# One load queue in the order of use, weights cast on VectorE, and an unrolled head of five units, in an HGRN2 attention followed by an MLP

## The chip, the cores and the metric

The kernel runs on one core of one Trainium2 chip. The metric is the device time of one execution in microseconds, and less is better. The engines are named as the profile names them: PE (TensorE, matmuls), DVE (VectorE), ACT (ScalarE), POOL (GpSimd), SP (SyncE, which issues DMAs here).

## The reference

A gated linear attention over 4 batches, 8 heads, 768 steps and a head size of 48, and then an MLP with a leaky ReLU over its 3072 rows of 384:

```python
# q, k, v, f_logit: (4, 8, 768, 48); w_in: (384, 2048); w_out: (2048, 384); all float32
f = 1.0 / (1.0 + np.exp(-f_logit))
state = np.zeros((B, H, D, D))
for t in range(S):
    state = f[:, :, t, :, None] * state + np.einsum('bhd,bhe->bhde', k[:, :, t], v[:, :, t])
    y[:, :, t] = np.einsum('bhd,bhde->bhe', q[:, :, t], state)
x = y.transpose(0, 2, 1, 3).reshape(B * S, H * D)
h = x @ w_in
out = np.maximum(0.01 * h, h) @ w_out
```

## The kernel before

The work is cut into 24 units, one for each chunk of 128 steps and each batch; the chunk is the outer index, so that units 0 to 3 are the first chunk of the four batches. One unit is 128 rows of the MLP's input. A unit goes through these steps, each a function of its own:

- `load(u)`: four DMAs of 192 KB on SP's queue (f, k, q, v, each 128 x 8 x 48 floats, so runs of 192 bytes).
- `gate_act` (ACT, L109 and L111): the negative logarithm of the gate. `gate_pe` (PE, L117 and L120): its running sum over the chunk in `cs`, by a triangular matrix, and four columns of totals. `decay_act` (ACT, L129 to L133): `em_t` and `a_t`, the exponentials of the sum and of its negative, and `a_end`.
- `scale_pool` (POOL, L139 to L142): `kh` = k times `em_t`, `qh` = q times `a_t`, and v in bf16.
- `turn_pe` and `turn_dve`: eight transposes into `tp`, copied to `kT` and to the block-diagonal `qbd` (DVE, L155 to L158).
- `score_pe` and `mask_dve`: scores in two PSUM tiles `pw`, masked into `wm` (DVE, L175).
- `mix_pe`, `y_act`: the unit's output `py` (L187 from the state, L191 within the chunk), copied to `xn` by ACT (L226). `state_pe`, `state_dve`, `state_pool`: the update of the batch's state (L203, L213 to L222).
- `x_pe`, `x_dve`: three transposes of `xn`, copied to `xT` (L233, L238).
- `up(u, g)`, g from 0 to 3: twelve matmuls with `xT` and a quarter of w_in's columns (L250), then the leaky ReLU on ACT into `gT` (L252).
- `down(u, half)`: eight matmuls with `gT` and w_out each (L259). `put(u)`: the copy to `osb` (DVE, L264) and the store on SP's queue.

The order is written out by hand: within an engine instructions run as the program lists them, and across engines they wait for each other's data and for buffers. PSUM tiles come from pools with few buffers: `sm` (`cs`, `py`, `pt` and `px` by turns) has two, `pw` two, `pm` two, `tp` one and `pm2` one.

Weights are loaded by POOL's queue, which casts float32 to bf16 on the way, in eight DMAs that are issued beside the first loads on SP's queue. Inputs are loaded five units ahead. Before the loop the attention of unit 0 is done; turn i of the loop then does the MLP of unit i with the attention of unit i + 1, the gate of unit i + 2 and the gate's logarithm of unit i + 3 between its pieces.

Of the kernel before, what the change touches and what calls it, by code (L numbers as in the profile page):

```python
# [9 lines left out]
FP32 = mybir.dt.float32  # L10
# [5 lines left out]
def kernel(  # L16
# [24 lines left out]
    const = ctx.enter_context(tc.tile_pool(name="const", bufs=1))  # L41
    inp = ctx.enter_context(tc.tile_pool(name="inp", bufs=6))
    work = ctx.enter_context(tc.tile_pool(name="work", bufs=3))
    gpool = ctx.enter_context(tc.tile_pool(name="gpool", bufs=5))
    opool = ctx.enter_context(tc.tile_pool(name="opool", bufs=4))

    ps_m = ctx.enter_context(tc.tile_pool(name="ps_m", bufs=2, space=bass.MemoryType.PSUM))
    ps_o = ctx.enter_context(tc.tile_pool(name="ps_o", bufs=1, space=bass.MemoryType.PSUM))
    ps_t = ctx.enter_context(tc.tile_pool(name="ps_t", bufs=1, space=bass.MemoryType.PSUM))
    ps_w = ctx.enter_context(tc.tile_pool(name="ps_w", bufs=2, space=bass.MemoryType.PSUM))  # L50
    ps_s = ctx.enter_context(tc.tile_pool(name="ps_s", bufs=2, space=bass.MemoryType.PSUM))

# [18 lines left out]
    qbds = [const.tile([128, P2, 2, 128], BF16, name=f"qbd{i}", tag=f"qbd{i}") for i in range(2)]  # L71
    state_f = [const.tile([128, P2, D], FP32, name=f"sf{b}", tag=f"sf{b}") for b in range(B)]
    state_b = [const.tile([128, P2, D], BF16, name=f"sb{b}", tag=f"sb{b}") for b in range(B)]
    for t in lfs + qhs + khs + qbds:
        nc.vector.memset(t, 0.0)
    for t in state_f:
        nc.vector.memset(t, 0.0)


    raw = {}  # L80
# [1 line left out]
    def load(u):  # L82
        c, b = units[u]
        r = {}
        for name, src in (("f", f_logit), ("k", k), ("q", q), ("v", v)):
            t = inp.tile([128, H, D], FP32, name=f"{name}_raw", tag=f"{name}_raw")
            nc.sync.dma_start(out=t, in_=src[b, :, c * C:(c + 1) * C, :].rearrange("h t d -> t h d"))
            r[name] = t
        raw[u] = r

    def load_w_in(part, parts):
        w = FF // parts
        for kk in range(NK):
            nc.gpsimd.dma_start(out=w_in_b[:, kk, part * w:(part + 1) * w],  # L94
                                in_=moe_w_in[kk * 128:(kk + 1) * 128, part * w:(part + 1) * w])

    def load_w_out(part, parts):
        n = NF // parts
        nc.gpsimd.dma_start(  # L99
            out=w_out_b[:, part * n:(part + 1) * n, :],  # L100
            in_=moe_w_out[part * n * 128:(part + 1) * n * 128, :].rearrange("(a p) n -> p a n", p=128))

    st = {}

# [1 line left out]
    def gate_act(u):  # L106
        f = raw[u]["f"]
        e = work.tile([128, H, D], FP32, name="e_t", tag="e_t")
        nc.scalar.activation(e, f, AF.Exp, scale=-1.0)  # L109
        lf = lfs[u % 3]  # L110
        nc.scalar.activation(lf[:, :, 0:D], e, AF.Ln, bias=1.0)  # L111

    def gate_pe(u):
        c, b = units[u]
        lf = lfs[u % 3]
        cs = ps_s.tile([128, 512], FP32, name="cs", tag="sm")
        nc.tensor.matmul(cs[:, 0:H * D], ut, lf[:, :, 0:D], start=True, stop=True)  # L117
        if c < NCH - 1:
            for p in range(P2):
                nc.tensor.matmul(cs[:, H * D + p:H * D + p + 1], lf[:, 2 * p:2 * p + 2, :], ones_col,  # L120
                                 start=True, stop=True)
        st[u] = {"cs": cs}

    def decay_act(u):
        c, b = units[u]
        cs = st[u]["cs"]
        a_t = work.tile([128, H, D], BF16, name="a_t", tag="a_t")
        em_t = work.tile([128, H, D], BF16, name="em_t", tag="em_t")
        nc.scalar.activation(em_t, cs[:, 0:H * D], AF.Exp, scale=1.0)  # L129
        nc.scalar.activation(a_t, cs[:, 0:H * D], AF.Exp, scale=-1.0)  # L130
        if c < NCH - 1:
            a_end = work.tile([128, P2], FP32, name="a_end", tag="a_end")
            nc.scalar.activation(a_end, cs[:, H * D:H * D + P2], AF.Exp, scale=-1.0)  # L133
            st[u]["a_end"] = a_end
        st[u]["a"], st[u]["em"] = a_t, em_t

    def scale_pool(u):
        r = raw.pop(u)
        nc.gpsimd.tensor_mul(khs[u % 3][:, :, 0:D], r["k"], st[u]["em"])  # L139
        nc.gpsimd.tensor_mul(qhs[u % 3][:, :, 0:D], r["q"], st[u]["a"])  # L140
        v_b = work.tile([128, H, D], BF16, name="v_b", tag="v_b")
        nc.gpsimd.tensor_copy(out=v_b, in_=r["v"])  # L142
        st[u]["v"] = v_b

    def turn_pe(u):
        tp = ps_t.tile([128, 2, P2, 128], BF16, name="tp", tag="tp")
        for i, src in enumerate((khs[u % 3], qhs[u % 3])):
            for p in range(P2):
                nc.tensor.transpose(tp[:, i, p, :], src[:, 2 * p:2 * p + 2, :], ident)  # L149
        st[u]["tp"] = tp  # L150

    def turn_dve(u):
        tp = st[u].pop("tp")
        kT = work.tile([128, P2, 128], BF16, name="kT", tag="kT")
        nc.vector.tensor_copy(out=kT, in_=tp[:, 0])  # L155
        qbd = qbds[u % 2]
        nc.vector.tensor_copy(out=qbd[0:64, :, 0, :], in_=tp[0:64, 1])
        nc.vector.tensor_copy(out=qbd[64:128, :, 1, :], in_=tp[64:128, 1])  # L158
        st[u]["kT"] = kT
# [91 lines left out]
                                 start=(kk == 0), stop=(kk == NK - 1))  # L251
        nc.scalar.activation(s["g"][:, 4 * g:4 * g + 4, :], pm, AF.Prelu, alpha=0.01)  # L252

    def down(u, half):
        s = st[u]
        if half == 0:
            s["pm2"] = ps_o.tile([128, KD], FP32, name="pm2", tag="pm2")
        for ff in range(8 * half, 8 * half + 8):
            nc.tensor.matmul(s["pm2"], s["g"][:, ff, :], w_out_b[:, ff, :], start=(ff == 0), stop=(ff == NF - 1))  # L259

    def put(u):
# [3 lines left out]
        nc.sync.dma_start(out=out[b * S + c * C:b * S + (c + 1) * C, :], in_=osb)  # L265
        st.pop(u)


    LA = 5
    load(0)  # L270
    load_w_in(0, 2)
    load(1)
    load_w_in(1, 2)
    load_w_out(0, 2)
    load_w_out(1, 2)
    for u in range(2, LA):
        load(u)

    gate_act(0)
    gate_act(1)  # L280
    gate_pe(0)
    decay_act(0)
    scale_pool(0)
    gate_pe(1)
    decay_act(1)
    scale_pool(1)
    gate_act(2)
    turn_pe(0)
    turn_dve(0)
    score_pe(0)  # L290
    mask_dve(0)
    mix_pe(0)
    state_pe(0)
    y_act(0)
    state_dve(0)
    state_pool(0)
    x_pe(0)
    x_dve(0)

    for i in range(NU):  # L300
        n1, n2, n3 = i + 1, i + 2, i + 3
        if i + LA < NU:
            load(i + LA)
        if n1 < NU:
            turn_pe(n1)
            turn_dve(n1)
        up(i, 0)
        up(i, 1)
        if n1 < NU:
            score_pe(n1)  # L310
            mask_dve(n1)
        if n2 < NU:
            gate_pe(n2)
            decay_act(n2)
            scale_pool(n2)
        up(i, 2)
        up(i, 3)
        if n1 < NU:
            mix_pe(n1)
            y_act(n1)  # L320
            state_pe(n1)
            state_dve(n1)
            state_pool(n1)
        if n3 < NU:
            gate_act(n3)
        down(i, 0)
        if n1 < NU:
            x_pe(n1)
            x_dve(n1)
        down(i, 1)  # L330
        put(i)

# [29 lines left out]
```

## Time and profile before

| | |
|---|---|
| median of 3 runs | 213.21 us (212.39 to 214.24) |
| the profiled execution | 211.29 us, its span 209.4 us |
| PE busy | 177.8 us, 85% of the span |
| DVE, ACT, POOL busy | 97.4, 108.7, 76.8 us |
| SP's queue (inputs, outputs) | 23.60 MB, 59.5% of 16 engines' span |
| POOL's queue (weights; bytes as written) | 3.15 MB, 9.0% |
| granted TensorE clock | 1.00 |

A line of the timeline has the start in us, the duration in us, the engine, the line of the kernel, the operation, the tile written and the tiles read, shapes, and the number of instructions merged in it; in brackets stands how long the engine had been idle and what ended that. A line of the chain of waits has start, duration, engine, tile and line. "x24" are 24 instructions. The page's rows of digits are the busy share of 40 equal slices, in tenths.

### The profile page before, as it was taken

What the parts mean: (1) busy time and instruction counts of PE and PEld (TensorE: products, weight loads), DVE (VectorE), ACT (ScalarE), POOL (GpSimd) and SP (SyncE); (2) the same over time, 40 slices, a digit from 0 to 9 for tenths busy, and PEclk for the clock granted to TensorE, in tenths of its full rate; (3) what the DMA queues carried; (4) which work ended last, traced back from release to release, by engine and by line L of the source; (5) the groups of instructions that cost most, each with busy time, mean ns of one, the idle gap of its engine ahead of it and who ended that gap; (6) DMA issues with size and microseconds to landing.
All of it is one profiled execution on the core that took longest, in us unless ns stands there. A gap on an engine that the chain in (4) does not pass through costs nothing.

```text
span 209.4 us, 5831 instructions
## 1 busy us (share of the span) xinstructions
PE 177.8 (85%) x2432; PEld 146.1 (70%) x2432; DVE 97.4 (46%) x223; ACT 108.7 (52%) x237; POOL 76.8 (37%) x129
## 2 busy tenths in 40 slices
PE   0000149999999999999999999999999999999993
PEld 0000028788779788877988887798888778877881
DVE  8000044466546545654654565465455545633511
ACT  4000332775576458447645845774585567555540
POOL 8300071542553255145325524532552454034000
PEclk9999999999999999999999999999999999999999
DMA  6999999998796479568647846956695681100111
GB/s 114 171 195 184 199 191 189 156 219 163 121 176 143 105 136 177 114 118 163 147 102 133 186 111 116 157 116 141 128 187 113 119 153 41 38 28 18 38 41 38
DMA packets 106267, 27.12 MB, mean 130 GB/s; under 512 B 100352, under 2 KB 105472, under 8 KB 106240
## 3 DMA queue, kind: packets, MB, share of 16 engines
q1 hardware_dynamic: 103296, 23.60, 59.5%
q0 software_dynamic: 2944, 3.15, 9.0%
q8 instruction: 19, 0.31, 0.6%
q14 instruction: 8, 0.07, 0.1%
HBM read 25.17 MB, written 4.72 MB: 143 GB/s over the span
## 4 chain that ended last, share of the span: by engine, by line
PE 83%; issue 10%; POOL 4%; DVE 1%; ACT 0%; POOLq 0%
PE pm L250 32%; PE pm L259 30%; PE pw L168 6%; PE tp L149 5%; PE py L191 2%; PE px L233 2%; PE py L187 2%; PE cs L117 2%; PE pt L203 2%; POOL w_in_b L94 2%; POOL w_out_b L99 1%; POOL kh L139 1%; PE cs L120 1%; DVE wm L175 1%; POOL qh L140 1%
## 5 line engine op out<-in xcount | busy, mean ns | idle before, releaser
L252 ACT ACTIVATE gT<-pm 128x512 bf16<-128x512 f32 x96 | 56.2, 601 | 64.1 <-PE pm L250 62.3
L250 PE MATMUL pm<-xT,w_in_b 128*128 128x128 bf16 x1152 | 73.4, 221 | 0.0
L259 PE MATMUL pm<-w_out_b,gT 128*128 128x384 bf16 x384 | 70.1, 326 | 0.0
L250 PEld LDWEIGHTS <-w_in_b 128*128 128x128 bf16 x1152 | 67.2, 99 | 0.6
L139 POOL TENSOR_TENSOR kh<-k_raw,em_t 128x384 bf16<-128x384 f32 x24 | 22.0, 916 | 110.5 <-ACT em_t L129 105.7
L259 PEld LDWEIGHTS <-gT 128*128 128x128 bf16 x384 | 35.2, 98 | 18.8
L175 DVE TENSOR_TENSOR wm<-pw,ut 128x512 bf16<-128x512 f32 x48 | 30.9, 686 | 12.7 <-PE pw L168 11.9
L117 PE MATMUL cs<-lf,ut 128*128 128x384 bf16 x24 | 8.1, 339 | 24.9 <-ACT lf L111 24.9
L264 DVE COPY osb<-pm 128x384 f32<-128x384 f32 x24 | 13.4, 558 | 26.6 <-PE pm L259 26.6
L109 ACT ACTIVATE e_t<-f_raw 128x384 f32<-128x384 f32 x24 | 12.9, 536 | 23.7 <-DMA f_raw<-in_f_logit_dram 23.7
L120 PEld LDWEIGHTS <-lf 128*128 128x128 bf16 x80 | 5.0, 99 | 25.2 <-issue 23.8
L140 POOL TENSOR_TENSOR qh<-q_raw,a_t 128x384 bf16<-128x384 f32 x24 | 21.9, 914 | 0.0
L155 DVE COPY kT<-tp 128x512 bf16<-128x512 bf16 x24 | 10.0, 415 | 23.6 <-PE tp L149 23.6
L238 DVE COPY xT<-px 128x384 bf16<-128x384 bf16 x24 | 8.6, 358 | 22.2 <-PE px L233 22.2
L213 DVE TENSOR_TENSOR sf<-sf,pt 64x192 f32<-64x192 f32 x20 | 6.9, 346 | 22.2 <-PE pt L203 22.2
L168 PE MATMUL pw<-qbd,kT 128*128 128x256 bf16 x96 | 14.8, 277 | 1.3 <-DVE qbd L158 1.3
L129 ACT ACTIVATE em_t<-cs 128x384 bf16<-128x384 f32 x24 | 11.8, 491 | 4.5 <-PE cs L120 3.7
L111 ACT ACTIVATE lf<-e_t 128x384 bf16<-128x384 f32 x24 | 12.5, 523 | 0.8
L168 PEld LDWEIGHTS <-kT 128*128 128x128 bf16 x96 | 9.4, 99 | 4.3 <-DVE kT L155 0.8
L226 ACT CAST xn<-py 128x384 bf16<-128x384 f32 x24 | 11.4, 474 | 1.5 <-PE py L191 1.5
L142 POOL CAST v_b<-v_raw 128x384 bf16<-128x384 f32 x24 | 12.1, 505 | 0.0
L130 ACT ACTIVATE a_t<-cs 128x384 bf16<-128x384 f32 x24 | 11.6, 485 | 0.0
(37 smaller groups left out, 155.3 us busy)
## 6 DMA issues: line engine op xcount, KB each, us to landing
f_raw<-in_f_logit_dram SPq DMA_DIRECT2D x24, 192.0 KB, 3.2
k_raw<-in_k_dram SPq DMA_DIRECT2D x24, 192.0 KB, 3.8
q_raw<-in_q_dram SPq DMA_DIRECT2D x24, 192.0 KB, 4.0
v_raw<-in_v_dram SPq DMA_DIRECT2D x24, 192.0 KB, 4.3
out_dram<-osb SPq DMA_DIRECT2D x24, 192.0 KB, 2.0
w_in_b<-in_moe_w_in_dram POOLq DMA_DIRECT2D x6, 256.0 KB, 8.8
w_out_b<-in_moe_w_out_dram POOLq DMA_DIRECT2D x2, 768.0 KB, 18.2
```

The lines of the kernel that those rows point to most:

```text
L109: nc.scalar.activation(e, f, AF.Exp, scale=-1.0)
L111: nc.scalar.activation(lf[:, :, 0:D], e, AF.Ln, bias=1.0)
L117: nc.tensor.matmul(cs[:, 0:H * D], ut, lf[:, :, 0:D], start=True, stop=True)
L139: nc.gpsimd.tensor_mul(khs[u % 3][:, :, 0:D], r["k"], st[u]["em"])
L140: nc.gpsimd.tensor_mul(qhs[u % 3][:, :, 0:D], r["q"], st[u]["a"])
L142: nc.gpsimd.tensor_copy(out=v_b, in_=r["v"])
L168: nc.tensor.matmul(pw[:, 2 * i:2 * i + 2, :], kT[:, p, :], qbd[:, p, :, :], start=True, stop=True)
L175: nc.vector.tensor_mul(wm, pw, ut[:, None, :].to_broadcast([128, 4, 128]))
L250: nc.tensor.matmul(pm[:, i, :], w_in_b[:, kk, ff * 128:(ff + 1) * 128], s["xT"][:, kk, :], start=(kk == 0), stop=(kk == NK - 1))
L252: nc.scalar.activation(s["g"][:, 4 * g:4 * g + 4, :], pm, AF.Prelu, alpha=0.01)
L259: nc.tensor.matmul(s["pm2"], s["g"][:, ff, :], w_out_b[:, ff, :], start=(ff == 0), stop=(ff == NF - 1))
L264: nc.vector.tensor_copy(out=osb, in_=st[u]["pm2"])
```

## The change

All loads are issued by SP, in one list. The weights come as float32 into staging tiles, w_in in four quarters of its columns and w_out in two halves of its columns, and DVE casts them into the bf16 tiles. The zeroing of the tiles is shared by DVE and POOL. For the first five units `kh` is made on DVE. `tp` takes its buffers from the pool of `pw`, and `pm2` has two banks. In place of the short prologue there is a head in which five units go through all their steps in an order written out by hand, with the down projection by halves of the output's columns (`down_cols`); the loop then begins at unit 5, whose first turn has an order of its own. Inputs are loaded four units ahead in the loop.

```diff
--- before.py
+++ after.py
@@ -41,12 +41,12 @@
     const = ctx.enter_context(tc.tile_pool(name="const", bufs=1))
     inp = ctx.enter_context(tc.tile_pool(name="inp", bufs=6))
     work = ctx.enter_context(tc.tile_pool(name="work", bufs=3))
-    gpool = ctx.enter_context(tc.tile_pool(name="gpool", bufs=5))
-    opool = ctx.enter_context(tc.tile_pool(name="opool", bufs=4))
+    gpool = ctx.enter_context(tc.tile_pool(name="gpool", bufs=6))
+    opool = ctx.enter_context(tc.tile_pool(name="opool", bufs=6))
+    stage = ctx.enter_context(tc.tile_pool(name="stage", bufs=1))
 
     ps_m = ctx.enter_context(tc.tile_pool(name="ps_m", bufs=2, space=bass.MemoryType.PSUM))
-    ps_o = ctx.enter_context(tc.tile_pool(name="ps_o", bufs=1, space=bass.MemoryType.PSUM))
-    ps_t = ctx.enter_context(tc.tile_pool(name="ps_t", bufs=1, space=bass.MemoryType.PSUM))
+    ps_o = ctx.enter_context(tc.tile_pool(name="ps_o", bufs=2, space=bass.MemoryType.PSUM))
     ps_w = ctx.enter_context(tc.tile_pool(name="ps_w", bufs=2, space=bass.MemoryType.PSUM))
     ps_s = ctx.enter_context(tc.tile_pool(name="ps_s", bufs=2, space=bass.MemoryType.PSUM))
 
@@ -71,10 +71,10 @@
     qbds = [const.tile([128, P2, 2, 128], BF16, name=f"qbd{i}", tag=f"qbd{i}") for i in range(2)]
     state_f = [const.tile([128, P2, D], FP32, name=f"sf{b}", tag=f"sf{b}") for b in range(B)]
     state_b = [const.tile([128, P2, D], BF16, name=f"sb{b}", tag=f"sb{b}") for b in range(B)]
-    for t in lfs + qhs + khs + qbds:
-        nc.vector.memset(t, 0.0)
+    for n, t in enumerate(lfs + khs + qhs + qbds):
+        (nc.vector if n % 2 == 0 else nc.gpsimd).memset(t, 0.0)
     for t in state_f:
-        nc.vector.memset(t, 0.0)
+        nc.gpsimd.memset(t, 0.0)
 
 
     raw = {}
@@ -88,17 +88,26 @@
             r[name] = t
         raw[u] = r
 
-    def load_w_in(part, parts):
-        w = FF // parts
-        for kk in range(NK):
-            nc.gpsimd.dma_start(out=w_in_b[:, kk, part * w:(part + 1) * w],
-                                in_=moe_w_in[kk * 128:(kk + 1) * 128, part * w:(part + 1) * w])
-
-    def load_w_out(part, parts):
-        n = NF // parts
-        nc.gpsimd.dma_start(
-            out=w_out_b[:, part * n:(part + 1) * n, :],
-            in_=moe_w_out[part * n * 128:(part + 1) * n * 128, :].rearrange("(a p) n -> p a n", p=128))
+    staged = {}
+
+    def load_w_in(part):
+        t = stage.tile([128, NK, 512], FP32, name=f"wi{part}", tag=f"wi{part}")
+        nc.sync.dma_start(out=t, in_=moe_w_in[:, part * 512:(part + 1) * 512].rearrange("(a p) n -> p a n", p=128))
+        staged["in", part] = t
+
+    def cast_w_in(part):
+        nc.vector.tensor_copy(out=w_in_b[:, :, part * 512:(part + 1) * 512], in_=staged["in", part])
+
+    def load_w_out(half):
+        t = stage.tile([128, NF, KD // 2], FP32, name=f"wo{half}", tag=f"wo{half}")
+        nc.sync.dma_start(
+            out=t, in_=moe_w_out[:, half * 192:(half + 1) * 192].rearrange("(a p) n -> p a n", p=128))
+        staged["out", half] = t
+
+    def cast_w_out(half):
+        for a in range(2):
+            nc.vector.tensor_copy(out=w_out_b[:, 8 * a:8 * a + 8, half * 192:(half + 1) * 192],
+                                  in_=staged["out", half][:, 8 * a:8 * a + 8, :])
 
     st = {}
 
@@ -134,16 +143,16 @@
             st[u]["a_end"] = a_end
         st[u]["a"], st[u]["em"] = a_t, em_t
 
-    def scale_pool(u):
+    def scale(u, k_on=None):
         r = raw.pop(u)
-        nc.gpsimd.tensor_mul(khs[u % 3][:, :, 0:D], r["k"], st[u]["em"])
+        (k_on or nc.gpsimd).tensor_mul(khs[u % 3][:, :, 0:D], r["k"], st[u]["em"])
         nc.gpsimd.tensor_mul(qhs[u % 3][:, :, 0:D], r["q"], st[u]["a"])
         v_b = work.tile([128, H, D], BF16, name="v_b", tag="v_b")
         nc.gpsimd.tensor_copy(out=v_b, in_=r["v"])
         st[u]["v"] = v_b
 
     def turn_pe(u):
-        tp = ps_t.tile([128, 2, P2, 128], BF16, name="tp", tag="tp")
+        tp = ps_w.tile([128, 2, P2, 128], BF16, name="tp", tag="pw")
         for i, src in enumerate((khs[u % 3], qhs[u % 3])):
             for p in range(P2):
                 nc.tensor.transpose(tp[:, i, p, :], src[:, 2 * p:2 * p + 2, :], ident)
@@ -251,11 +260,11 @@
                                  start=(kk == 0), stop=(kk == NK - 1))
         nc.scalar.activation(s["g"][:, 4 * g:4 * g + 4, :], pm, AF.Prelu, alpha=0.01)
 
-    def down(u, half):
+    def down(u, part):
         s = st[u]
-        if half == 0:
+        if part == 0:
             s["pm2"] = ps_o.tile([128, KD], FP32, name="pm2", tag="pm2")
-        for ff in range(8 * half, 8 * half + 8):
+        for ff in range(8 * part, 8 * part + 8):
             nc.tensor.matmul(s["pm2"], s["g"][:, ff, :], w_out_b[:, ff, :], start=(ff == 0), stop=(ff == NF - 1))
 
     def put(u):
@@ -265,60 +274,147 @@
         nc.sync.dma_start(out=out[b * S + c * C:b * S + (c + 1) * C, :], in_=osb)
         st.pop(u)
 
-
-    LA = 5
-    load(0)
-    load_w_in(0, 2)
-    load(1)
-    load_w_in(1, 2)
-    load_w_out(0, 2)
-    load_w_out(1, 2)
-    for u in range(2, LA):
-        load(u)
+    def down_cols(u, half):
+
+        c, b = units[u]
+        s = st[u]
+        if half == 0:
+            s["o"] = opool.tile([128, KD], FP32, name="osb", tag="osb")
+        cols = slice(half * 192, (half + 1) * 192)
+        pm2 = ps_o.tile([128, KD], FP32, name="pm2", tag="pm2")
+        for ff in range(NF):
+            nc.tensor.matmul(pm2[:, 0:192], s["g"][:, ff, :], w_out_b[:, ff, cols], start=(ff == 0), stop=(ff == NF - 1))
+        nc.vector.tensor_copy(out=s["o"][:, cols], in_=pm2[:, 0:192])
+        if half == 1:
+            nc.sync.dma_start(out=out[b * S + c * C:b * S + (c + 1) * C, :], in_=s["o"])
+            st.pop(u)
+
+
+    HEAD = 5
+    for x in ("u0", "u1", "u2", "i0", "i1", "u3", "i2", "i3", "u4", "o0", "o1", "u5"):
+        {"u": load, "i": load_w_in, "o": load_w_out}[x[0]](int(x[1]))
+
+    def turn(u):
+        turn_pe(u)
+        turn_dve(u)
+
+    def score(u):
+        score_pe(u)
+        mask_dve(u)
+
+    def gate(u, k_on=None):
+        gate_pe(u)
+        decay_act(u)
+        scale(u, k_on)
+
+    def mix(u):
+        mix_pe(u)
+        y_act(u)
+        state_pe(u)
+
+    def xturn(u):
+        x_pe(u)
+        x_dve(u)
+        state_dve(u)
+        state_pool(u)
+
 
     gate_act(0)
+    gate(0, nc.vector)
     gate_act(1)
-    gate_pe(0)
-    decay_act(0)
-    scale_pool(0)
-    gate_pe(1)
-    decay_act(1)
-    scale_pool(1)
+    turn(0)
+    gate(1, nc.vector)
+    score(0)
     gate_act(2)
-    turn_pe(0)
-    turn_dve(0)
-    score_pe(0)
-    mask_dve(0)
-    mix_pe(0)
-    state_pe(0)
-    y_act(0)
-    state_dve(0)
-    state_pool(0)
-    x_pe(0)
-    x_dve(0)
-
-    for i in range(NU):
+    mix(0)
+    turn(1)
+    xturn(0)
+    gate(2, nc.vector)
+    score(1)
+    mix(1)
+    turn(2)
+    xturn(1)
+    cast_w_in(0)
+    score(2)
+    up(0, 0)
+    up(1, 0)
+    mix(2)
+    xturn(2)
+    cast_w_in(1)
+    up(2, 0)
+    up(0, 1)
+    up(1, 1)
+    up(2, 1)
+    gate_act(3)
+    gate(3, nc.vector)
+    turn(3)
+    score(3)
+    cast_w_in(2)
+    up(0, 2)
+    mix(3)
+    up(1, 2)
+    xturn(3)
+    up(2, 2)
+    cast_w_in(3)
+    for g in range(3):
+        up(3, g)
+    for u in range(4):
+        up(u, 3)
+    gate_act(4)
+    gate(4, nc.vector)
+    turn(4)
+    score(4)
+    mix(4)
+    xturn(4)
+    for g in range(4):
+        up(4, g)
+    cast_w_out(0)
+    for u in range(3):
+        down_cols(u, 0)
+    gate_act(5)
+    down_cols(3, 0)
+    down_cols(4, 0)
+    cast_w_out(1)
+    gate(5)
+    load(6)
+    load(7)
+    load(8)
+    down_cols(0, 1)
+    down_cols(1, 1)
+    turn(5)
+    down_cols(2, 1)
+    score(5)
+    down_cols(3, 1)
+    mix(5)
+    gate_act(6)
+    down_cols(4, 1)
+    xturn(5)
+
+    for i in range(HEAD, NU):
         n1, n2, n3 = i + 1, i + 2, i + 3
-        if i + LA < NU:
-            load(i + LA)
-        if n1 < NU:
-            turn_pe(n1)
-            turn_dve(n1)
+        if i + 4 < NU:
+            load(i + 4)
+        if i == HEAD:
+            gate(n1)
+        if n1 < NU and i > HEAD:
+            turn(n1)
         up(i, 0)
         up(i, 1)
+        if i == HEAD:
+            turn(n1)
+            gate_act(n2)
+        if n1 < NU and i > HEAD:
+            score(n1)
+        if n2 < NU and i > HEAD:
+            gate(n2)
+        up(i, 2)
+        if i == HEAD:
+            score(n1)
+        up(i, 3)
+        if i == HEAD:
+            gate(n2)
         if n1 < NU:
-            score_pe(n1)
-            mask_dve(n1)
-        if n2 < NU:
-            gate_pe(n2)
-            decay_act(n2)
-            scale_pool(n2)
-        up(i, 2)
-        up(i, 3)
-        if n1 < NU:
-            mix_pe(n1)
-            y_act(n1)
-            state_pe(n1)
+            mix(n1)
             state_dve(n1)
             state_pool(n1)
         if n3 < NU:
```

## The prediction

> **What bounds the kernel now.** I read the page's 40 slices first, then the chain of waits, then the timeline of the head. The first fence has three lines of the page:
>
> ```profile
> span 209.4 us, 5831 instructions
> ...
> PE   0000149999999999999999999999999999999993
> ...
> DMA  6999999998796479568647846956695681100111
> ```
>
> A slice is 5.2 us. PE does nearly nothing for six slices and is then full to the end. So only two things can move the end: when the full stretch begins, and how much of it is lost again. The chain of waits, in order of time, gives what one unit costs once PE is full:
>
> ```profile
> 63.20 0.45 PE tp L149 x8
> 63.64 1.34 PE pm L250 x24
> ...
> 70.50 0.45 PE tp L149 x8
> 70.95 1.34 PE pm L250 x24
> ```
>
> From one unit's first up-projection to the next one's is 70.95 - 63.64 = 7.31 us, and unit 5 starts its own at 70.95. From there to the end of the span are 209.4 - 70.95 = 138.45 us. After its unrolled head the changed kernel runs the same loop from unit 5 on, so I look for one number, X: when `up(5, 0)` starts. The timeline of the head shows why PE starts late, and what a unit's attention costs on the way to it:
>
> ```profile
> 3.73 0.52 ACT L109 ACTIVATE e_t<-f_raw 128x384 f32<-128x384 f32 x1 [1.71 <-DMA f_raw<-in_f_logit_dram]
> ...
> 24.35 0.52 ACT L109 ACTIVATE e_t<-f_raw 128x384 f32<-128x384 f32 x1 [19.54 <-DMA f_raw<-in_f_logit_dram]
> ...
> 25.33 0.47 ACT L129 ACTIVATE em_t<-cs 128x384 bf16<-128x384 f32 x1
> ...
> 26.76 0.91 POOL L140 TENSOR_TENSOR qh<-q_raw,a_t 128x384 bf16<-128x384 f32 x1
> ...
> 30.33 1.29 DVE L175 TENSOR_TENSOR wm<-pw,ut 128x512 bf16<-128x512 f32 x2 [0.75 <-POOL v_b L142]
> ...
> 32.05 0.48 ACT L226 CAST xn<-py 128x384 bf16<-128x384 f32 x1 [1.45 <-PE py L191]
> ...
> 33.12 0.36 DVE L238 COPY xT<-px 128x384 bf16<-128x384 bf16 x1
> ...
> 33.73 2.77 PE L250 MATMUL pm<-xT,w_in_b 128*128 128x128 bf16 x24
> ...
> 37.05 1.50 PE L250 MATMUL pm<-xT,w_in_b 128*128 128x128 bf16 x24
> ```
>
> Unit 1's gate input is issued early and lands at 24.3, because the weights in POOL's queue share the engines. Then follows pure latency: 8.15 us from `em_t` (25.33) to the end of `xT` (33.48), through POOL, PE, DVE, PE, DVE, PE, ACT, PE, DVE. The last two lines show that 24 matmuls take 2.77 us after the idle stretch and 1.50 us once PE has worked for some 3.7 us, though the granted clock is printed as 1.00 in both.
>
> **The change part by part: the loads.** Back to back, SP issues a 192 KB load every 0.98 us (from 26.65 to 33.20 it issues seven). The first landed at 3.7. In the new order the inputs of units 0, 1, 2 are in at 6.6, 10.6, 14.5. The output stores bound the weights' rate from above: 192 KB each in 1536-byte packets, 65 ns in the median of the trace's records of them, or 24 GB/s per engine, 378 over sixteen. The loads' 196.6 kB in 0.98 us, 200 GB/s, bounds it from below. A quarter of w_in (786 kB) is then 2.1 to 3.9 us, a half of w_out (1573 kB) 4.2 to 7.9. I take 2.1 and 4.7, since rows of 2 KB and 768 bytes are nearer the stores. So the quarters are in at 16.6, 18.6, 24.6 and 26.7, unit 4 at 30.6, the halves at 35 and 40. At the dear price these are 18.5, 22, 30, 34, 38, 46 and 54. Either way they are earlier than the uses found below (23.8, 30.2, 41.3, 47.5, 62, 72.9), so the queue costs nothing; DVE's order is its cover.
>
> **DVE's order.** DVE takes its instructions as written. `cast_w_in(0)` stands behind `state_dve(1)`, `cast_w_in(1)` behind `state_dve(2)`, `cast_w_in(2)` behind `mask_dve(3)`, and `cast_w_out(1)` behind the copy of `down_cols(4, 0)`. A cast is 128x1536, f32 to bf16. From above: `osb` 384 in 0.558 and `wm` 512 in 0.686 give 1.0 ns per element, 1.71 us. From below: `xT` 384 in 0.358 and `kT` 512 in 0.415 give 0.45 ns, 0.87 us. I take 1.0, near the lower end, because these casts read no PSUM as both of the upper rows do. [...]
>
> **The first three units.** Durations are those of the lines above: `e_t` and `lf` 1.04; `cs` with its four columns 0.77; `em_t` 0.49 and `a_t` 0.37 later; `qh` 0.91 on POOL; four transposes 0.61, eight 1.1; the three copies of `turn_dve` 1.21; scores 1.0; masks 1.29; `py` and `pt` 0.85; `xn` 0.48; `px` 0.5; `xT` 0.36; `state_dve` 0.7. `kh` on DVE is 0.55 (between `sf` 0.35 for 192 and `wm` 0.69 for 512; on POOL 0.92) and hides behind `qh`. The memsets split between DVE and POOL end at about 6, before POOL's first `qh`. Unit 0: gate input 3.7, `em_t` 6.1, `qh` 7.5, `qbd` 9.4; `gate(1)` is ahead of `score(0)` on PE (9.5); scores 10.5, masks 12.0, `xn` 13.1, transposes of unit 1 14.0, `xT` 15.6, `state_dve` 16.3. The `sm` pool has two buffers, so `cs` of unit 2 waits for `state_dve(0)`, and `score(1)` is queued behind it on PE. That gives scores 18.1, masks 19.6, `xT` 23.1, `state_dve(1)` 23.8, cast 24.8. Two `up` at the slow rate of the row (2.56 us for two in the chain) end at 27.4, `mix(2)` at 28.5, `xT` 29.5, `state_dve(2)` 30.2, cast 31.2, three `up` at 0.67 end at 33.3, and ACT is free at 33.9.
>
> **Two lone chains.** `gate_act(3)` stands on ACT behind the leaky-ReLU of `up(2, 1)`, though its input came at 19.6, and PE's next instructions all need the chain's results. From 33.9: `lf` 35.0, `cs` 35.8, `qh` 37.6, `qbd` 39.4, masks 41.3, cast 42.3, `up(0, 2)` from 42.35. PE is all but idle for 9 us. The `up` run then begins slow, and ends at 51.8 (seven more after `cast_w_in(2)` and `xT` of unit 3, then four). `gate_act(4)` waits behind the last of these too, on ACT, to 52.4, and the same chain with `xn`, `px` and `xT` ends at 61.4: 9 us more, in which `down_cols` can't go ahead, as PE has `up(4, ...)` first. Four `up`, 2.9 of them slow, end at 65.8. Five `down_cols` at 1.33 (192 columns, between 56 ns for 128 and 163 for 384) end at 72.5; then the copy and the whole second cast, half of it under the first eight matmuls, leave PE waiting until 74.95. Five second halves with unit 5's turn, score and mix between them end at 82.9; `xT` and `state_dve(5)`, for which `cs` of unit 6 waits, at 84.1; `up(5, 0)` starts at 84.6.
>
> **The loop's first turn.** `gate(6)` stands just ahead of it, where before the turn of unit 6 was done too. Added: turn 0.45, its wait for `qh` 0.9, the wait for `qbd` 0.6, and `pt` waiting for ACT to read `cs` of unit 7, 0.8: 2.8 us. After that the turns are alike. Split columns cost PE no more (32 at 83 ns against 16 at 163). The second `pm2` bank and `tp` in the shared pool free nothing that the 7.31 us wait for.
>
> **Sum.** 84.6 + 138.45 + 2.8 = 225.9, against 209.4: 16.5 more. The profiled execution took 211.29, 1.9 beyond its span, so 227.8 on its own scale. The median of the runs, 213.21, is 1.9 above that execution; on their scale it is 229.7. I say 229, between the two, nearer the runs.
>
> [...] I priced each burst by the row; without it X would be about 5 us earlier, which speaks for the low side.
>
> **The rivals.** (1) Slower, but less: casts at 0.87, PE never slow again. X is 78.5, the time about 223. For it: no second burst is in this trace. Against: PE stayed slow from 26.85 to 36, working half of the time. (2) Slower still: casts at 1.71 on five places (+3.6) and every burst slow to its end (+3): 235. (3) The lone chains hide: if ACT and DVE get ahead of the `up` run, the two gaps of 8.5 and 9.0 vanish, X is 67.1, the span 208.4, the time 210 to 212, within 1% or just faster. Against: the order within ACT. (4) Faster: the head is bound by the loads alone. The second half of w_out is in at 40, cast at 41, first halves done by then, 8.4 us of second halves with unit 5, 1.5 for `xT`, state and gate: X about 54, span 195, time 198. It decides once chains of different units overlap wholly; the early start of PE at 25 instead of 34 speaks for it. (5) The change doesn't do what it says, one queue being slower for weights: at the dear price above still nothing, and the time is that of the forecast.
>
> **How the numbers follow.** Forecast and its near neighbours (224 to 232) 0.55, rival 1 0.15, rival 2 0.13, rival 3 0.08, rival 4 0.09. A 1% difference is about what a measurement of this kernel can tell from none. Faster by over 1%: rival 4 and a third of rival 3, 0.12; within 1%: 0.05; slower: 0.83. The range 215 to 236 takes in the two slower rivals.
>
> **What would show it.** After: PE's slices thin until the 13th or so, with two gaps of about 9 us (near 34 and 52) that end at `wm` or `xT` of a single unit; ACT's `e_t` of units 3 and 4 long after their landing; DVE's casts on the chain and not waiting for a DMA; `up(5, 0)` near 85; 7.3 us a unit thereafter. Wrong if `e_t` of unit 3 runs beside the `up` of quarter 1, if PE is full from 30 on, or if a cast waits for its load.

## The result, and the profile after

The changed kernel is slower. Its median is 232.49 us (231.71 to 233.06), against 212.8 for the kernel before in the same comparison; the ratio is 1.0913, with a 95% interval of 1.0845 to 1.098. The forecast was 229, within 215 to 236. The profiled execution took 232.54 us with a span of 230.8; the span before was 209.4, so 21.4 us have been added between these two executions (19.7 between the medians), where the sum said 16.5.

The page first: the span, PE's 40 slices, the granted clock and the DMA share.

```profile
span 230.8 us, 6002 instructions
...
PE   0465672594599696799999999999999999999994
...
PEclk9999977589559799999999999999999999999999
DMA  7999989999000017256588556866678475710100
```

PE does real work from the second slice on (5.8 us each), where before it read 0 for four of 5.2, but it does not stay at 9 until the eighteenth. Two holes stand out, the seventh slice and the tenth and eleventh, and around them the granted clock falls to 5 to 7 tenths, where before it was 9 in every slice. The DMA row is at 9 through the first hole and at 0 from the eleventh to the fourteenth slice, so whether a load or something else makes the holes has to be read elsewhere. The chain of waits, in order of time, shows what the first hole is made of:

```profile
31.07 3.58 PE pm L259 x36
34.67 0.60 ACT gT L261
35.27 0.42 ACT e_t L118
35.72 0.53 ACT lf L120
36.29 0.32 PE cs L126
36.73 0.49 ACT em_t L138
37.22 0.38 ACT a_t L139
37.68 0.92 POOL qh L149
38.65 0.62 PE tp L158 x4
39.29 0.42 DVE kT L164
39.72 0.33 DVE qbd L166
40.07 0.44 DVE qbd L167
40.55 0.60 PE pw L177 x2
41.17 1.29 DVE wm L184 x2
42.46 1.67 DVE w_in_b L99
44.18 1.46 PE pm L259 x12
...
99.58 1.34 PE pm L259 x24
...
106.88 1.34 PE pm L259 x24
```

`gate_act(3)` follows the last leaky-ReLU of quarter 1 on ACT (`gT`, 34.67), and from there one unit's attention runs alone from engine to engine, each with one instruction at a time and hardly anything beside it, until the cast behind `wm` lets `up(0, 2)` start at 44.18. The last two lines are the loop: 7.30 us from `up(6, 0)` to `up(7, 0)`, as before.

Ahead of these lines the chain runs through SP's issues and a load (`22.11 7.13 DMA k_raw`), and the page therefore gives 9% of the span to SP's queue and 3% to this load. That step is no wait: it is the load of unit 4's k, which landed at 29.24, 0.02 before the cast of quarter 1 began, but this cast reads a load that was issued at 12.81 and took at most 6.9 us to land, and DVE was busy until 29.23. The timeline carries the sizes (start, busy, engine, operation, count, and the idle time before it with its releaser):

```profile
22.26 1.75 DVE L99 CAST w_in_b<-wi 128x1536 bf16<-128x1536 f32 x1
...
24.07 2.74 PE L259 MATMUL pm<-xT,w_in_b 128*128 128x128 bf16 x24 [1.79 <-DVE w_in_b L99]
...
54.26 0.51 ACT L118 ACTIVATE e_t<-f_raw 128x384 f32<-128x384 f32 x1
...
63.34 5.12 PE L259 MATMUL pm<-xT,w_in_b 128*128 128x128 bf16 x48 [0.45 <-DVE xT L247]
...
75.37 2.54 DVE L109 CAST w_out_b<-wo 128x1536 bf16<-128x1536 f32 x2
...
77.96 3.63 PE L286 MATMUL pm<-w_out_b,gT 128*128 128x192 bf16 x24 [0.77 <-DVE w_out_b L109]
...
88.30 1.50 PE L259 MATMUL pm<-xT,w_in_b 128*128 128x128 bf16 x24
```

The second lone chain runs from 54.26 to 63.34. `up(5, 0)`, the X of the prediction, starts at 88.30. The windows put the engines side by side over the two chains and what follows them (columns: stretch, length, then busy time and count of PE, its weight loads, DVE, ACT and POOL, the granted clock, DMA share, GB/s):

```profile
35.00:44.00 9.00, 2.63 (x17) 1.44 (x16) 4.56 (x7) 2.15 (x6) 1.36 (x2) 0.63 1.19 312
...
54.00:63.00 9.00, 4.11 (x40) 2.73 (x40) 3.10 (x7) 2.71 (x7) 1.36 (x2) 0.72 0.49 72
63.00:69.00 6.00, 5.66 (x57) 5.66 (x57) 3.03 (x5) 2.30 (x5) 2.16 (x2) 0.57 0.00 0
```

No engine is busy for much over half of a chain's 9 us: this is latency. And in the six microseconds behind the second chain PE is nearly full, but at a mean clock of 0.57.

### The profile page after: what moved, and what is told of

The parts are those of the page before. It is cut to its first block, busy times and chain, and to the rows that moved or that the text cites. A ratio compares the mean times of both kernels' runs of the same rounds, so it can differ in the third digit from the quotient of the medians.

```text
span 230.8 us, 6002 instructions
## 1 busy us (share of the span) xinstructions
PE 193.3 (84%) x2512; PEld 161.1 (70%) x2512; DVE 109.8 (48%) x232; ACT 109.9 (48%) x237; POOL 73.3 (32%) x125
## 4 chain that ended last, share of the span: by engine, by line
PE 74%; SPq 9%; DVE 6%; DMA 3%; ACT 3%; POOL 2%; issue 1%; POOLq 0%
PE pm L259 29%; PE pm L268 21%; SPq L87 8%; PE pm L286 6%; PE pw L177 5%; PE tp L158 4%; DMA k_raw<-in_k_dram 3%; PE py L200 2%; PE py L196 2%; PE px L242 2%; DVE w_in_b L99 1%; PE cs L126 1%; PE pt L212 1%; SPq L95 1%; POOL qh L149 1%
## 5 line engine op out<-in xcount | busy, mean ns | idle before, releaser
L259 PE MATMUL pm<-xT,w_in_b 128*128 128x128 bf16 x1152 | 78.5, 229 | 6.9 <-DVE w_in_b L99 6.0
L259 PEld LDWEIGHTS <-w_in_b 128*128 128x128 bf16 x1152 | 72.2, 103 | 9.4 <-DVE w_in_b L99 7.3
L268 PE MATMUL pm<-w_out_b,gT 128*128 128x384 bf16 x304 | 55.4, 326 | 0.0
L148 POOL TENSOR_TENSOR kh<-k_raw,em_t 128x384 bf16<-128x384 f32 x19 | 17.7, 930 | 80.5 <-ACT em_t L138 75.7
L268 PEld LDWEIGHTS <-gT 128*128 128x128 bf16 x304 | 27.8, 98 | 14.9
L230 POOL TENSOR_TENSOR sf<-sf,a_end 128x192 f32<-128x192 f32 x20 | 10.8, 541 | 39.4 <-DVE sf L223 39.4
L273 DVE COPY osb<-pm 128x384 f32<-128x384 f32 x19 | 10.6, 558 | 21.8 <-PE pm L268 21.8
L177 PE MATMUL pw<-qbd,kT 128*128 128x256 bf16 x96 | 16.4, 300 | 4.2 <-DVE qbd L167 4.2
L286 PE MATMUL pm<-w_out_b,gT 128*128 128x192 bf16 x160 | 15.7, 260 | 1.8 <-DVE w_out_b L109 1.8
L286 PEld LDWEIGHTS <-gT 128*128 128x128 bf16 x160 | 14.4, 104 | 2.2 <-issue 2.1
L158 PE MATMUL tp<-ident,kh 128*128 128x128 bf16 x96 | 10.4, 238 | 4.5 <-DVE kh L148 3.6
```

Of the source, the lines that this page charges most:

```text
L148: (k_on or nc.gpsimd).tensor_mul(khs[u % 3][:, :, 0:D], r["k"], st[u]["em"])
L177: nc.tensor.matmul(pw[:, 2 * i:2 * i + 2, :], kT[:, p, :], qbd[:, p, :, :], start=True, stop=True)
L259: nc.tensor.matmul(pm[:, i, :], w_in_b[:, kk, ff * 128:(ff + 1) * 128], s["xT"][:, kk, :], start=(kk == 0), stop=(kk == NK - 1))
L286: nc.tensor.matmul(pm2[:, 0:192], s["g"][:, ff, :], w_out_b[:, ff, cols], start=(ff == 0), stop=(ff == NF - 1))
```

## The experiments

Theory A puts the loss in the order of the head: lone chains, the clock that falls in them, casts that are dearer than 1.0 us, and an end of the head (called the tail below) that leaves unit 6's turn to the loop. Theory B puts it in the loads and casts: one queue, f32 over the wire, and conversion on DVE. Theory C, in the first two runs, puts it in the slow clock alone. For the runs on the changed kernel I compare the start of `up(6, 0)`: 78.25 in the kernel before (70.95 + 7.30), 99.58 in the changed one, 21.3 later:

```profile
78.25 1.34 PE pm L250 x24
```

What comes after is alike. Each start is that of one profiled execution, and the runs were on different chips; the changed kernel's own spans run from 229.9 to 231.3, so a difference of 1 us means little. Ratios are to the kernel before, on the same chip and over several executions; where the two disagree, the text gives both.

**One chain taken into other work.** Unit 3's parts are started earlier in the written order; nothing else is touched.

```diff
     mix(2)
+    gate_act(3)
     xturn(2)
     cast_w_in(1)
     up(2, 0)
+    gate(3, nc.vector)
     up(0, 1)
+    turn(3)
     up(1, 1)
     up(2, 1)
-    gate_act(3)
-    gate(3, nc.vector)
-    turn(3)
     score(3)
```

> The changed kernel with unit 3's gate, turn and score moved between the up-projections of quarter 1, so that its chain no longer stands alone. Theory A (the time is lost in latency: each engine takes its list in order, and two lone chains of units 3 and 4 leave PE idle for 9.5 us each): the first use of quarter 2 moves from 44.2 to about 38.5 (the cast still stands behind the masks), 5 to 7 us less, about 226. Theory B (the weights' new way, loads and casts, sets the pace): nothing, 232. Theory C (the slow clock of PE after gaps is the loss): 1 to 2 us less.

Measured: 225.39 us, ratio 1.0546 (1.048 to 1.0613), as A expected; C had expected 1 to 2 us. `up(6, 0)` starts at 93.50, 6.1 earlier. Of the 9.5 us of the hole not all is won, because `cast_w_in(2)` still stands behind unit 3's masks on DVE:

```profile
38.57 1.46 PE L259 MATMUL pm<-xT,w_in_b 128*128 128x128 bf16 x12 [2.83 <-DVE w_in_b L99]
```

**Both chains.** The same for unit 4, spread over the `up` of units 0 to 3.

```diff
-    for g in range(3):
-        up(3, g)
-    for u in range(4):
-        up(u, 3)
     gate_act(4)
+    up(3, 0)
     gate(4, nc.vector)
+    up(3, 1)
+    up(3, 2)
     turn(4)
+    up(0, 3)
+    up(1, 3)
     score(4)
+    up(2, 3)
     mix(4)
+    up(3, 3)
     xturn(4)
```

> The same, and unit 4's chain laid between the up-projections of units 3 and of quarter 3 as well. Theory A: the second lone gap (53.8 to 63.3) goes too, 9 us more, about 217 in all, so some 15 of the 20 us that the change cost. Theory B: 230 to 232. Theory C: about 228.

Measured: 217.45 us, ratio 1.0153 (1.0084 to 1.0222), again as A expected, `up(6, 0)` at 82.59: 17.0 us of the 21.3 are gone, with no change to a load, a cast or a matmul. The profiled execution was the fastest of the four; by the ratios 7.6 of the 9.1 points are gone, about the same share. The clock came back with it (0.999 in the mean of this execution and 0.984 in the others, against 0.941), and `up(4, ...)` takes 3.02 us where it took 5.12:

```profile
50.10 3.02 PE L259 MATMUL pm<-xT,w_in_b 128*128 128x128 bf16 x48 [0.45 <-DVE xT L247]
...
82.59 1.34 PE pm L259 x24
```

**The clock by itself.** The chains stay, but PE is given useless matmuls in their gaps (9, 6, 7 and 14 around unit 3's parts; 9, 6, 7, 4, 2 and 2 around unit 4's). Their output goes into a `pm2` bank that nobody reads.

```diff
+    def fill(n):
+        t = ps_o.tile([128, KD], FP32, name="pm2", tag="pm2")
+        for _ in range(n):
+            nc.tensor.matmul(t, ident, w_in_b[:, 0, 0:KD], start=True, stop=True)
...
     gate_act(3)
+    fill(9)
     gate(3, nc.vector)
+    fill(6)
     turn(3)
+    fill(7)
     score(3)
+    fill(14)
     cast_w_in(2)
...
```

> The changed kernel with matmuls of no use laid into the gaps of PE during the chains of units 3 and 4, so that PE does not rest; they add to no result. If the granted clock, 0.59 to 0.70 in those stretches, costs what the first row of the kernel before priced, the four up-projections of unit 4 take 2.9 us instead of 5.1, those after the cast of quarter 2 some 1.5 less, and each chain about 0.5: 4 to 5 us less, 228. If the slow clock costs nothing of note: 232, or more by what the fillers delay.

Measured: 226.92 us, ratio 1.0708 (1.0657 to 1.0759); the span is 225.5, 5.3 less than that of the changed kernel, though PE does more. The page's clock row, and the timeline of the `up` behind the two chains:

```profile
PEclk9999999999999999999999999999999999999999
```

```profile
44.56 0.84 PE L259 MATMUL pm<-xT,w_in_b 128*128 128x128 bf16 x12 [0.55 <-DVE w_in_b L99]
...
61.78 3.02 PE L259 MATMUL pm<-xT,w_in_b 128*128 128x128 bf16 x48
```

So the slow clock in and after the chains costs about 5 us (5.3 between the spans, 2.05 points or 4.4 us by the ratios). The run with both chains taken in avoids it as well: it is a part of those 17.0, not an addition. That leaves, by subtraction, some 12 of the 17.0 for time in which PE had nothing to do.

**The layout of the casts.** `w_in_b` is laid out by quarters, so that each cast of w_in writes one run of 1536 elements instead of three of 512.

```diff
-    w_in_b = const.tile([128, NK, FF], BF16, tag="w_in")
+    w_in_b = const.tile([128, 4, NK, 512], BF16, tag="w_in")
...
-        nc.vector.tensor_copy(out=w_in_b[:, :, part * 512:(part + 1) * 512], in_=staged["in", part])
+        nc.vector.tensor_copy(out=w_in_b[:, part], in_=staged["in", part])
...
```

> The changed kernel with the bf16 tile of w_in laid out by quarters, so that a cast writes 1536 elements without a break; nothing else changes. The cast of a w_in quarter took 1.75 us and that of 8 x 192 elements of w_out, as many, 1.07. If the broken rows of the destination (3 runs of 512) are what makes the first slow, a cast takes 1.0 to 1.1 us, and the three on the path give 2.0 us, 230.4. If the rate belongs to the data from w_in or to their place in time, the cast stays at 1.75 and the time at 232.5.

Measured: 229.76 us, ratio 1.0754 (1.0691 to 1.0818), `up(6, 0)` 3.1 us earlier. The cast of the same 1536 elements now takes

```profile
45.63 0.96 DVE L99 CAST w_in_b<-wi 128x1536 bf16<-128x1536 f32 x1
...
96.44 1.34 PE pm L259 x24
```

against 1.75 in the changed kernel. Three casts on the path by 0.79 are 2.4. The other 0.7 lies in the rate of PE: the 36 matmuls of quarter 1 took 2.36 us here (66 ns each) against 3.57 (99 ns) in the changed kernel, whose granted clock was 0.50 from 30.7 to 33.9, and smaller delays take back a part of that 1.2. Whether the shorter wait for the cast kept the rate up, or chance did, no run shows.

**The tail.** The second half of w_out is cast right after the first `down_cols`; `gate(6)`, `gate_act(7)` and `turn(6)` go between the last `down_cols`, so that the loop's first turn is like the others. For this, unit 5's parts stand one or two `down_cols` earlier too.

```diff
-    for u in range(3):
+    down_cols(0, 0)
+    cast_w_out(1)
+    for u in range(1, 3):
         down_cols(u, 0)
...
+    xturn(5)
+    gate(6)
+    down_cols(3, 1)
+    gate_act(7)
     down_cols(4, 1)
-    xturn(5)
+    turn(6)
...
-        if i == HEAD:
-            turn(n1)
-            gate_act(n2)
```

> The changed kernel with the end of its head alone as in b4: the cast of w_out's second half among the first down-projections, unit 5 a little earlier, unit 6's gate and turn inside the head. The wait for the cast (75.1 to 78.0 in the changed kernel, 2.9 us less a copy), the wait of unit 6's sum for unit 5's state (0.9) and the long first turn of the loop (11.3 against 7.3, of which 0.7 is work that only moves) go: 6 to 7 us less, 226. If these waits were covered by the lone chains' slack: 1 to 2 us.

Measured: 227.81 us, ratio 1.0785 (1.0723 to 1.0847), `up(6, 0)` at 94.48, 5.1 us earlier:

```profile
94.48 1.34 PE pm L259 x24
```

By the ratios it is 1.3 points, or 2.7 us, so its size is less sure than that of the chains. Both are under the 6 to 7 us that were expected. The trace names a part of what is missing: `turn(5)` now waits 0.23 and 0.47 us for POOL.

**The loads alone.** The kernel before with the new loads (units 0 and 1, four quarters of w_in, unit 2, two halves of w_out, all on SP's queue), casts on DVE, and the old loop. The quarters are cast behind `x_dve(0)`, the halves behind unit 1's masks.

```diff
-    load_w_in(0, 2)
-    load_w_in(1, 2)
-    load_w_out(0, 2)
-    load_w_out(1, 2)
+    for part in range(4):
+        load_w_in(part)
+    load(2)
+    load_w_out(0)
+    load_w_out(1)
...
+    for part in range(4):
+        cast_w_in(part)
...
+        if i == 0:
+            cast_w_out(0)
+            cast_w_out(1)
```

> The kernel before with the loads of the change alone: one queue on SP, weights as float32 by quarters and halves, cast by DVE (quarters after unit 0's input of the MLP, halves after the masks of unit 1); no unrolled head, pools and memsets as before. Theory A: the new way of the weights is no loss and even a gain by itself. By the landings of the changed kernel (a quarter some 2 us, a half 4.7) w_out is in at about 32.5 and cast at 34, so unit 0's first down-projection starts near 34 against 38.9: 4 to 5 us faster than before, 208. Theory B: slower than before, 216 or more.

Measured: 210.91 us, ratio 0.985 (0.9776 to 0.9924). The loads and casts cost nothing in the old order of work; they gain. B falls as the cause of the loss. The gain is smaller than expected: the first matmul of w_out starts at 36.94 instead of 34, because unit 2's gate input lands at 20.60 and on ACT it stands ahead of unit 0's `xn`:

```profile
20.60 0.52 ACT L119 ACTIVATE e_t<-f_raw 128x384 f32<-128x384 f32 x1 [9.84 <-DMA f_raw<-in_f_logit_dram]
...
21.59 0.46 ACT L236 CAST xn<-py 128x384 bf16<-128x384 f32 x1
```

**The head alone.** The changed kernel's head with the weights loaded as before, in POOL's queue and without casts.

```diff
-    cast_w_in(0)
...
-    for x in ("u0", "u1", "u2", "i0", "i1", "u3", "i2", "i3", "u4", "o0", "o1", "u5"):
-        {"u": load, "i": load_w_in, "o": load_w_out}[x[0]](int(x[1]))
+    load(0)
+    load_w_in(0, 2)
+    load(1)
+    load_w_in(1, 2)
+    load_w_out(0, 2)
+    load_w_out(1, 2)
+    for u in range(2, 6):
+        load(u)
```

> The changed kernel's unrolled head with the weights loaded as before: POOL's queue, cast on the way, no casts on DVE, the order of the loads as before. Theory A (latency of chains in a fixed order): the head waits for the inputs of units 1 and 2, which came at 24.3 and 29.5 beside the weights, so the first up-projection starts near 38.5 against 24.1; the waits for casts go (about 9 us): 236 to 240. Theory B (the new way of the weights is the loss): 212 or less.

Measured: 236.28 us, ratio 1.1133 (1.1067 to 1.1199). The new order with the old loads is the worst of all, as unit 2's gate input comes late and PE's first `up` starts at 38.73, later than the 33.73 of the kernel before:

```profile
29.61 0.52 ACT L108 ACTIVATE e_t<-f_raw 128x384 f32<-128x384 f32 x1 [16.12 <-DMA f_raw<-in_f_logit_dram]
...
38.73 2.76 PE L249 MATMUL pm<-xT,w_in_b 128*128 128x128 bf16 x24
```

Together with the run before it this splits the change in two: its loads are worth 1.5% taken alone, its order of work costs 11% taken alone. Of these 11%, 5.0 us are PE's later first `up`: the new order needs the new loads.

**Better loads, twice.** On the loads alone, unit 2 is moved ahead of the quarters and the layout by quarters is taken. In the first of two runs the casts of w_out also stood ahead of unit 1's masks on DVE.

```diff
+    load(2)
     for part in range(4):
         load_w_in(part)
-    load(2)
...
         if i == 0:
             cast_w_out(0)
             cast_w_out(1)
         if n1 < NU:
             score_pe(n1)
             mask_dve(n1)
```

> The kernel before with the new loads alone, as in a4, but unit 2's inputs ahead of the weights (in a4 its gate on ACT waited for them until 20.6 and held unit 0's xn behind it for 5 us) and w_in's bf16 tile laid out by quarters. Unit 0's first down-projection then starts at about 33.5 instead of 36.9, when the first part of w_out's second half is cast: 207.5. If the load of w_out sets it, not less than 207; if PE's work is what counts, 211 as in a4.

Measured: 212.09 us, ratio 1.0021 (0.9995 to 1.0047): a miss. DVE waits twice for a load, and the masks of unit 1, on which PE waits, stand behind both waits:

```profile
28.18 3.25 DVE L110 CAST w_out_b<-wo 128x1536 bf16<-128x1536 f32 x2 [2.14 <-DMA wo<-in_moe_w_out_dram]
...
33.58 1.83 DVE L110 CAST w_out_b<-wo 128x1536 bf16<-128x1536 f32 x2 [2.15 <-DMA wo<-in_moe_w_out_dram]
35.44 1.29 DVE L185 TENSOR_TENSOR wm<-pw,ut 128x512 bf16<-128x512 f32 x2
```

In the second run the two casts go behind the masks again, and nothing else is changed.

> b3 once more, with the casts of w_out behind unit 1's masks on DVE, as they stood in a4. In b3 they stood ahead of the masks, and DVE waited for the loads of w_out's halves (idle before 28.2 and before 33.6), so unit 1's masks came at 35.4. Behind the masks, unit 0's first down-projection starts when the first part of the second half is cast, near 34.5 against 37.25: 2.5 to 3 us less than b3, 1 to 1.5% below the kernel before. If the wait for w_out itself is what counts, no gain over b3.

Measured: 208.94 us, ratio 0.9888 (0.9836 to 0.9941). The same two casts, moved by one place on one engine, are worth 1.3% by the ratios (3.7 us between the two profiled spans, 210.5 and 206.8, which were on different chips). The first w_out matmul starts at 34.18, now behind w_out's own landing and cast.

**All together.** Both chains taken in, the layout, the tail, and in addition `cast_w_in(2)` ahead of `score(3)`, `gate_act(4)` two `up` earlier, `mix(3)` and `xturn(3)` one `up` later, `cast_w_out(0)` ahead of `up(4, ...)`, and most of unit 5's parts one `down_cols` earlier again. The diff shows some of this.

```diff
+    turn(3)
+    cast_w_in(2)
     up(1, 1)
     up(2, 1)
...
     score(3)
-    cast_w_in(2)
...
+    down_cols(0, 0)
+    cast_w_out(1)
+    down_cols(1, 0)
+    gate(5)
+    down_cols(2, 0)
...
```

> The changed kernel with every loss that the trace names taken out: both lone chains between the up-projections, w_in laid out by quarters, the cast of quarter 2 ahead of unit 3's masks, the cast of w_out's second half early among the first down-projections, and unit 6's gate and turn inside the head, so that the loop's first turn is like the others. Theory A: the loop starts its up-projections near 64 and runs on as before: 205 to 206, faster than the kernel before by 3 to 4%. If something else in the unrolled head costs (split down-projections, shared PSUM), 210 or more.

Measured: 207.72 us, ratio 0.9808 (0.9766 to 0.9849): below the kernel before. `up(6, 0)` starts at 74.41, 25.2 us earlier than in the changed kernel:

```profile
74.41 1.34 PE pm L259 x24
```

The three single edits gave 17.0 + 3.1 + 5.1 = 25.2; by the ratios they gave 7.6 + 1.6 + 1.3 = 10.5 points, and all together 11.05. So the sum closes to within the noise: the unrolled head would be 3.8 us ahead of the old one, and the three losses turn that into 21.3 behind. (This version has the small moves that the single edits lack, and the clock is in two of the three terms, so that the agreement to the tenth is luck.) X is 67.1, some 3 us later than expected. Half of that is the slow first burst, which the next run takes away (X there is 65.6); for the rest I found no single wait, and it stays open.

**All, with the gaps filled.** Into the gaps of the first three chains go 33 useless matmuls of 128 columns (8, 8, 8 and 9).

```diff
+            nc.tensor.matmul(t[:, 0:128], ident, ut, start=True, stop=True)
...
+    fill(8)
```

> b4 with fillers of no use on PE in the gaps of the first three units' chains (33 matmuls of 128 columns, 1 us or less in each gap; they add to no result), so that PE's clock is granted in full when the first up-projections start. In b4 the first 24 matmuls took 2.74 us against 1.50. If the clock is the cause: 1.50 here, and 1.2 us less in all, 0.6% below b4. If what follows waits for DVE anyway: no change of the time.

Measured: 206.08 us, ratio 0.9754 (0.9678 to 0.983). The span is 204.2 against 205.6 (on another chip; the two ratios' intervals overlap), and the first 24 matmuls of `up` take 1.51 us, where the changed kernel's took 2.74:

```profile
22.96 1.51 PE L259 MATMUL pm<-xT,w_in_b 128*128 128x128 bf16 x24 [0.91 <-DVE w_in_b L99]
```

This is the best version found, 2.5% below the kernel before. The matmuls are not fast throughout: the mean clock of this execution was 0.992, and 12 and 24 matmuls of `up` that began at 27.95 and 30.29 took 1.32 and 2.11 us, against 0.83 for 12 at 26.32 and 1.51 for 24 at 32.79.

## Why the prediction was right, and where its sizes were off

The mechanism was the one forecast: the loop from unit 5 on is unchanged, and all that is added lies ahead of `up(6, 0)`. Following the sum's own steps (predicted, then measured):

| step | predicted | measured | running difference |
|---|---|---|---|
| first `w_in` cast starts | 23.8 | 22.26 | -1.5 |
| unit 3's lone chain starts (`e_t`) | 33.9 | 35.17 | +1.3 |
| `up(0, 2)` starts | 42.35 | 44.18 | +1.8 |
| unit 4's lone chain starts (`e_t`) | 52.4 | 54.26 | +1.9 |
| `up(4, 0)` starts | 61.4 | 63.34 | +1.9 |
| second halves go on behind w_out's second cast | 74.95 | 77.96 | +3.0 |
| `up(5, 0)`, X | 84.6 | 88.30 | +3.7 |
| added in the loop's first turn | 2.8 | 99.58 - 88.30 - 7.31 = 3.97 | +4.9 in all |

- **The lone chains** were right in place, cause and size: 8.45 and 9.0 predicted, 9.0 (35.17 to 44.18) and 9.1 measured, with 0.74 more for the cast in the first. That they are the main cause is shown by taking them away: 17.0 of 21.3 us, the slow clock included.
- **The loads** cost nothing, as said: no cast in the changed kernel has idle time of DVE ahead of it that a DMA ended, and PE's first `up` comes at 24.07 instead of 33.73. Rival 5 is settled by the run with the loads alone.
- **The cast of a quarter of w_in** is the term that was mis-sized: taken at 1.0, it is 1.75. The upper bound of 1.71 from rows that read PSUM was nearer than the lower one, and the argument for the lower one (these casts read no PSUM) did not hold for this destination; no row had shown it either, as `xT` and `kT`, from which the lower bound came, read PSUM too. Three of them on the path make +2.25. For a quarter of w_in, a time near 1.0 came only when the layout made the destination one run (0.96).
- **The clock** was priced too low. The sum let a burst recover early; the 36 matmuls of quarter 1 took 3.57 instead of 2.0, `up(4, ...)` 5.12 instead of 4.4, and the 24 matmuls behind the second cast 3.63 instead of about 2.0 (24 at 83 ns), together 3.9 us. The estimate that the later bursts' slowness is worth "about 5 us" agrees in size with the 5.3 that filling the gaps gave, but not term by term: of the 5.3, 1.5 are the 24 matmuls behind the second cast, which the sum took at full rate. That PE is slow again after a later gap was the author's estimate in the sum, priced by the one slow row of the kernel before (2.77 against 1.50 us for 24 matmuls); no row there shows a second slow burst. The changed kernel does: between 27 and 84 us its granted clock fell to 0.50 four times, and PE had no gap longer than 2.62 us in that time. So rival 1, no second slow phase, was wrong; rival 2, everything dear, came nearest in size: 235 against 232.5.
- **What went the other way**: units 0 to 2 were 1.5 us faster than worked out, and from the second halves to X the rest took 0.9 less (10.34 in all with the slow 24 matmuls, 9.65 predicted). 2.25 + 3.9 - 1.5 - 0.9 is 3.75, about the 3.7 by which X was missed; the loop's first turn adds 1.2. That the forecast lies as near as 3.5 us is partly luck, since the errors have both signs.
- **Rival 3**, chains that hide, was not what the order gives, but it is what the order can be made to give: 217.45, or 207.72 with the other two losses out, against the 210 to 212 that it named.
- **Rival 4**, bound by the loads at 198, was never reached. With the old order and the masks ahead of the casts, w_out's landing does set when its matmuls start, at 34.18 us.

## What to carry to other kernels

When a prologue is unrolled so that an engine starts earlier, follow each in-order engine's list through the seam: a unit's first small step that is written behind another unit's last one (here `gate_act` behind the leaky-ReLU) makes the whole latency of its chain bare, 9 us each time, and the fix is to move a few lines, not to load faster. A conversion written into the list of an engine that others wait for belongs behind the step that PE waits for, not ahead of it; for the two casts of w_out this was worth 1.3%. Where a busy engine gets holes, price the work after the hole at its slow rate too: here some 5 of the 17 us that the holes cost were the clock.

## What the runs showed of the hardware that was not expected

**The shape of a cast's destination.** 1536 elements from f32 to bf16 within SBUF took 1.75 us into three runs of 512, 0.91 or 0.92 into eight runs of 192 where POOL was idle (1.82 and 1.83 for a pair), and 0.96 into one run. Why three runs are slow, and one run and eight are not, no run shows: only three runs against one was varied by an experiment, and the casts into eight runs are those of w_out.

**POOL beside a fast cast.** In the run with the casts behind the masks, the first pair of w_out casts took 3.25 us and the second, of the same shape, 1.83. Beside the first, POOL's `qh`, 0.91 elsewhere, took 1.63, and its `v_b` cast, 0.50 elsewhere, 1.23. From its timeline:

```profile
27.94 3.25 DVE L110 CAST w_out_b<-wo 128x1536 bf16<-128x1536 f32 x2 [0.18 <-DMA wo<-in_moe_w_out_dram]
28.73 1.63 POOL L150 TENSOR_TENSOR qh<-q_raw,a_t 128x384 bf16<-128x384 f32 x1
...
33.17 1.83 DVE L110 CAST w_out_b<-wo 128x1536 bf16<-128x1536 f32 x2 [1.98 <-DMA wo<-in_moe_w_out_dram]
```

Two comparisons show what goes with what. The run with the new layout differs from the changed kernel in nothing but the layout of w_in's bf16 tile, and by it in the rate of w_in's casts. Beside the slow cast (22.26, 1.75 us) POOL's `sf` takes its usual 0.51; beside the fast one it ends only 0.36 us after the cast. The first line is the changed kernel's, the others are of the run with the new layout:

```profile
22.31 0.51 POOL L230 TENSOR_TENSOR sf<-sf,a_end 128x192 f32<-128x192 f32 x1 [3.71 <-DVE sf L223]
...
22.40 0.96 DVE L99 CAST w_in_b<-wi 128x1536 bf16<-128x1536 f32 x1
22.45 1.27 POOL L230 TENSOR_TENSOR sf<-sf,a_end 128x192 f32<-128x192 f32 x1 [3.71 <-DVE sf L223]
```

And the second pair of w_out casts, 2.54 us in the changed kernel beside POOL's `kh` (1.19) and `qh` (1.63), takes 1.82 in the run of the tail, where POOL has nothing to do beside it. So POOL's `sf` is longer beside the fast cast (1.27 us against 0.51), and the pair of w_out casts is longer beside POOL's `kh` and `qh` (2.54 against 1.82). By what means, no run shows.

**The granted clock.** It does not tell all: before the change it read 1.00 while the first 24 matmuls of `up` took 2.77 us instead of 1.50. The trace holds its first record of the clock only at 36.4 us there, and at 27.2 us in the changed kernel, where the matmuls turn fast, so the 1.00 ahead of that is no reading. In the changed kernel the mean was 0.63 and 0.72 over stretches in which PE was 29 and 46% busy, and lowest, 0.57, in the nearly full stretch behind them. These means mix two values: cut finer, it is 0.50 from 30.7 to 33.9, 37.5 to 47.6, 58.0 to 68.0 and 78.5 to 81.7 us, and 1.00 between them. In the 3 us ahead of each fall PE was busy for 0.5 to 1.4 us. So a burst can be slow because of the stretch ahead of it, though PE is full in the burst itself: with the gaps of unit 3's and unit 4's chains filled, `up(4, ...)` took 3.02 us against 5.12. Nor does the mean of a whole execution follow its time: the changed kernel's four executions had 0.941 three times and 0.985 once, and the span of that one, 229.9 us, was only 0.7 to 1.4 us shorter.
